# Doubled spectrum products and tap diagonals read by quadrants from PSUM in a fused S4 convolution and mixture-of-experts kernel

## The chip, the cores and the metric

One core of one Trainium2 chip. The metric is the device time of one execution in microseconds (us); "span" is the time from the first to the last instruction in the profile and is 1.8 to 2.1 us shorter in these runs. Engines: PE (TensorE matmul), PEld (its weight loads), DVE (VectorE), ACT (ScalarE), POOL, SP. The record calls a run slow when it is over 1.5% above the fastest of its kernel; all figures below are medians or means of the fast runs.

## The reference, cut to what matters

```python
g = sigmoid((x * gate_w).sum(-1, keepdims=True))      # x: 2048 tokens, 512 channels
a = ssm(x)                                            # S4: long convolution, one kernel per channel
b = moe(x)                                            # top-2 tokens go through one gated MLP
return g * a + (1 - g) * b

def ssm(u):                                           # D = 512 channels, N = 128 states
    logdA = exp(log_dt)[:, None] * (A_re + 1j * A_im)
    K  = einsum("dn,dnl,dn->dl", C, exp(logdA[:, :, None] * arange(2048)), dt * B).real
    Yf = rfft(pad(u)) * rfft(pad(K))                  # length 4096
    return irfft(Yf)[:2048] + u * Dskip
```

The kernel works on the channels in two halves of HC = 256, and each half in NG = 64 groups of four channels. A half passes through these stages:

- **Tables** of powers of the discretised A are made on DVE and ACT.
- **Taps**: for each group two matmuls (real and imaginary table) give a 128 x 84 tile. Its rows are 32 values of s for each of 4 channels, its columns 21 slots for each of 4 channels. Only the *diagonal* is wanted, where row and column belong to the same channel (the index c4).
- **Spectrum of K** ("Kh") by matmul from the diagonal rows, then eviction from PSUM.
- **Products** of the spectra of K and of u (X) on DVE, sums, folds, and the inverse transform on PE.

## The kernel before

A view `t(BF, p0, np, col, (stride, n), ...)` is: type, first partition, number of partitions, first column, then pairs of stride and count. `g.op(name, {engine: (code, cost)}, reads, writes)` records an operation. At build time a list scheduler in the kernel turns the operations into one fixed issue order per engine, by priorities from a table (ORDER), engine choices from another (ENGINE) and the order in which tiles get their addresses (PLACE).

```python
# taps: six groups to a PSUM bank, then one wide eviction
hh.matmul(o, tT1[h](BF, 0, 128, gr * 128, (1, 128)), ..., start=True, stop=False)
r = hh.matmul(o, tTI[h](BF, 0, 128, gr * 128, (1, 128)), ..., start=False, stop=True)
# ... (cut)
g.op("ev tap ...", {ACT: ..., DVE: ...})            # 128 x 1008 from PSUM to tKA, bf16

# selection: a 0/1 matrix picks the diagonal of tKA and puts it into rows 32*qd + s
for c4 in range(4):
    for qd, s in enumerate(slots):
        r = hh.matmul(ps(F32, 32 * qd, 32, (tl - tl0) * 256 + c4, (4, NG)), tSM(BF, 0, 128, 256 + 32 * c4, (1, 32)),
                      tKA(BF, 0, 128, s * 4 + c4, (84, NG)), start=True, stop=True, tile_position=(0, 32 * qd))
# ... and two more evictions, "ev kc" and "ev kd", into tKC

# products: one operation for each pair of a K part and an X part
def prod(nm, kb, kri, b, xri):                       # kri, xri: 0 = real, 1 = imaginary
    t = T(nm, NE * 2); bt = Buf(t)
    tt(nm, lambda: f4(t), lambda: k4(kb, kri), lambda: xw(b, xri), ALU.mult,
       bKH[h][kb * 4 + kri * 2:kb * 4 + kri * 2 + 2] + bX[b][xri], [bt], cd(NE), bias)
    return t, bt
```

The list before the output buffer `[bt]` says what a product has to wait for: half of a spectrum, either the real or the imaginary part.

## Time and profile before

| | before |
|---|---|
| device time | 163.69 us (163.63 to 163.76) |
| profiled execution | span 163.2 us, device time 164.97 us |
| DVE busy | 149.9 us, 228 instructions |
| PE busy | 146.2 us, 1574 matmuls |
| ACT busy | 123.8 us, 242 instructions |

"Busy" is the time in which at least one instruction of the engine runs. The profiled execution was 1.3 us slower than the timed ones. The lines of this profile stand in the prediction. One line of its DVE timeline (start, length, engine, line, operation, count) is added: the last stretch of products and folds, 73 of them.

```profile
107.29 48.95 DVE L664 TENSOR_TENSOR RB<-RB 128x2048 bf16<-128x2048 bf16 x73
```

### The profile page before, as it was taken

The numbers are of one execution on the slowest core, as the hardware profiler recorded it, in microseconds if no ns is written. First come the engines' busy times: TensorE is split into PE (matmuls) and PEld (weight loads), VectorE is DVE, ScalarE is ACT, GpSimd is POOL, SyncE is SP. The second block draws the span as 40 slices with busy tenths as digits, with TensorE's granted clock in tenths as the row PEclk, the third lists the DMA queues.
The fourth block names the chain that finished last, engine by engine and source line by source line (L and its number), as shares of the span: only waits on it lengthen the run. The fifth ranks groups of instructions, "written<-read, shape, count | busy, mean of one in ns | idle before, by whom it ended". The sixth has DMA issues, their size and how long they took to land.

```text
span 163.2 us, 3756 instructions
## 1 busy us (share of the span) xinstructions
PE 146.2 (90%) x1574; PEld 102.4 (63%) x1574; DVE 149.9 (92%) x228; ACT 123.8 (76%) x242; POOL 4.2 (3%) x12
## 2 busy tenths in 40 slices
PE   0588899999799999849999999999999999999991
PEld 0443545464334457748555679998588888888880
DVE  0499999999999999999998999999999999999933
ACT  3698999999998998999998989974751602562352
POOL 5000000000000000000100000000000000000000
PEclk9999999999999999858999999999999999999999
DMA  4899600000000996596152504858000000044044
GB/s 148 257 378 416 209 7 0 4 4 0 0 0 3 324 352 227 187 349 242 39 222 38 221 4 159 359 181 335 2 0 6 0 0 4 0 129 133 0 129 129
DMA packets 13300, 21.19 MB, mean 130 GB/s; under 512 B 2018, under 2 KB 10980, under 8 KB 12516
## 3 DMA queue, kind: packets, MB, share of 16 engines
q1 hardware_dynamic: 12996, 20.93, 37.2%
q8 instruction: 12, 0.20, 0.5%
q10 hardware_dynamic: 288, 0.03, 0.1%
q14 instruction: 4, 0.03, 0.1%
HBM read 18.86 MB, written 2.10 MB: 128 GB/s over the span
## 4 chain that ended last, share of the span: by engine, by line
PE 57%; ACT 20%; DVE 16%; DMA 3%; SPq 1%; issue 1%; DVEq 0%
PE RP L1253 17%; PE RP L958 14%; DVE RB L664 10%; PE RP L788 6%; ACT RB L851 6%; ACT RB L768 5%; ACT RB L689 5%; PE RP L844 4%; PE RP L925 4%; DMA RB<-in_A_B_re_dram 3%; PE RP L1250 2%; ACT RB L990 2%; PE RP L1227 2%; PE RP L1147 2%; DVE RB L686 2%; PE RP L898 1%
## 5 line engine op out<-in xcount | busy, mean ns | idle before, releaser
L664 DVE TENSOR_TENSOR RB<-RB 128x2048 bf16<-128x2048 bf16 (+4 forms) x103 | 83.0, 870 | 1.3 <-ACT RB L792 0.8
L844 PE MATMUL RP<-RB 128*128 128x512 bf16 x128 | 31.3, 380 | 2.8 <-ACT RB L851 1.4
L1253 PE MATMUL RP<-RB 128*128 128x256 bf16 x256 | 32.0, 273 | 0.0
L1253 PEld LDWEIGHTS RP<-RB 128*128 128x128 bf16 x256 | 25.0, 98 | 3.0 <-issue 0.2
L958 PE MATMUL RP<-RB 128*128 128x256 bf16 x208 | 25.0, 273 | 0.0
L963 ACT ACTIVATE RB<-RP 128x1024 bf16<-128x1024 f32 x14 | 14.2, 1042 | 13.7 <-PE RP L958 13.7
L708 DVE TENSOR_TENSOR RB<-RB 128x2048 bf16<-128x2048 bf16 x20 | 23.8, 1218 | 0.1
L958 PEld LDWEIGHTS RP<-RB 128*128 128x128 bf16 x208 | 20.1, 98 | 4.5 <-issue 0.2
L844 PEld LDWEIGHTS RP<-RB 128*128 128x128 bf16 x128 | 11.7, 97 | 17.6 <-ACT RB L851 3.3
L1266 ACT ACTIVATE RB<-RP,RB 128x256 bf16<-128x256 f32 x28 | 10.8, 487 | 12.0 <-DVE RB L664 5.5
L792 ACT ACTIVATE RB<-RP 128x512 bf16<-128x512 int16 x32 | 18.4, 610 | 1.5 <-PE RP L788 1.3
L768 ACT ACTIVATE RB<-RP 128x256 bf16<-128x256 f32 x62 | 18.9, 507 | 0.0
L851 ACT ACTIVATE RB<-RP 128x1024 bf16<-128x1024 f32 x15 | 15.4, 1079 | 0.4 <-PE RP L847 0.3
L788 PE MATMUL RP<-RB 128*128 128x512 bf16 x56 | 15.5, 380 | 0.0
L898 PE MATMUL RP<-RB 128*128 128x84 bf16 x128 | 11.8, 213 | 3.5 <-DVE RB L664 3.1
L898 PEld LDWEIGHTS RP<-RB 128*128 128x128 bf16 x128 | 11.2, 105 | 4.0 <-DVE RB L664 3.2
L710 DVE TENSOR_TENSOR RB<-RB 128x1024 bf16<-128x1024 bf16 x20 | 13.4, 683 | 0.0
L899 PE MATMUL RP<-RB 128*128 128x84 bf16 x128 | 11.8, 212 | 0.0
L899 PEld LDWEIGHTS RP<-RB 128*128 128x128 bf16 x128 | 11.3, 105 | 0.0
L689 ACT ACTIVATE RB<-RB 128x512 bf16<-128x512 int16 x16 | 9.1, 626 | 0.5 <-DVE RB L686 0.5
L913 ACT ACTIVATE RB<-RP 128x1008 bf16<-128x1008 f32 x9 | 9.0, 1046 | 0.0
L1250 PE MATMUL RP<-RB 128*128 128x256 bf16 x32 | 8.8, 274 | 0.0
(106 smaller groups left out, 161.1 us busy)
## 6 DMA issues: line engine op xcount, KB each, us to landing
RB<-in_A_u_dram SPq DMA_DIRECT2D x4, 1024.0 KB, 6.0
RB<-c_kspec SPq DMA_DIRECT2D x6, 512.0 KB, 4.6
RB<-c_fwd SPq DMA_DIRECT2D x4, 512.0 KB, 9.1
RB<-c_inv SPq DMA_DIRECT2D x2, 1024.0 KB, 6.6
RB<-in_B_w_up_dram SPq DMA_DIRECT2D x2, 896.0 KB, 6.9
RB<-in_B_w_gate_dram SPq DMA_DIRECT2D x2, 896.0 KB, 6.0
RB<-in_B_w_down_dram SPq DMA_DIRECT2D x2, 896.0 KB, 6.1
out_dram<-RB SPq DMA_DIRECT2D x6, 256.0 KB, 2.4
```

The source lines that it names most:

```text
L664: return g.op(name, {DVE: (lambda h: h.tensor_tensor(out=o(), in0=a(), in1=b(), op=op), cost)}, rd, wr, bias=bias, **kw)
L689: s1.append(g.op("sin z%d.%d" % (t, hh_), {ACT: (lambda h, ta=ta, i=i, hh_=hh_: h.activation(out=tZ[hh_](BF, 0, 128, i * 512, (256, 2), (1 ...
L708: g.op("%s.m%d" % (name, i), {DVE: (lambda h, i=i: h.tensor_tensor(out=ts[i](BF, 0, 128, 0, (n, 2), *like), in0=a_(), in1=b_(i), op=ALU.mu ...
L768: e2.append(g.op("exp t1_%d %d" % (h, m), {ACT: (lambda hh, m=m, s=s, h=h: hh.activation(out=tT1[h](BF, 0, 128, s * 4, (128, NG), (1, 4)), ...
L788: r = hh.matmul(ps(F32, 0, 128, 0, (1, 512)), tAM(BF, 0, 128, 1 * 128, (1, 128)), tU8(BF, 0, 128, (x * 2 + h) * HC, (0, 2), (1, HC)), star ...
L792: sins.append(g.op("sin%d %d.%d" % (h, q, cs), {ACT: (lambda hh, ps=ps, cs=cs, tt_=tt_, q=q: hh.activation(out=tt_(BF, 0, 128, 8 * q, (4, ...
L844: r = h.matmul(o, tF(BF, 0, 128, (((eo * 2 + ri) * 4 + j // 2) * 4 + ft) * 128, (1, 128)), tU(BF, 0, 128, (b * 8 + j) * D, (1, D)), start= ...
L851: g.op("ev X%d.%d.%d" % (b, ri, pr), {ACT: (lambda h, ps=ps, b=b, pr=pr, ri=ri: h.activation(out=eov(b, ri, 2 * pr, (1, 1024)), in_=ps(F32 ...
L898: hh.matmul(o, tT1[h](BF, 0, 128, gr * 128, (1, 128)), t2v(h, 0, 0, (HC, NSL), (1, 4)) if gr == 0 else tT2[h](BF, 0, 128, 4 * gr, (HC, NSL ...
L899: r = hh.matmul(o, tTI[h](BF, 0, 128, gr * 128, (1, 128)), tT2[h](BF, 0, 128, NSL * HC + 4 * gr, (HC, NSL), (1, 4)), start=False, stop=True)
L958: r = hh.matmul(o, tKM[m](BF, 0, 128, c, (1, 128)), tKC[h](BF, 0, 128, u * 256, (1, 256)), start=(n == 0), stop=(n == len(steps) - 1))
L1253: r = hh.matmul(o, tG(BF, 0, 128, ((j * 2 + ri) * 4 + ft) * 128, (1, 128)), SD(hb, ri, ft), start=False, stop=(fin and k == 1 and ft == r0 ...
```

## The change

Its intent is to shorten both full engines: fewer and larger DVE products, no selection on PE. The parts are: (1) a product takes the real and the imaginary part of K at once (and, with them, both parts of X); (2) the weights of the taps are read at stride 4, so that the rows of a tap tile are ordered by channel first, and each diagonal is then one quadrant (32 partitions) of PSUM that ACT or DVE copies straight into its rows; (3) the selection and its evictions go; (4) each of four table products (the D products) is split in two; (5) loads at the start are reordered; (6) a new ORDER, ENGINE and PLACE. Cut to its core:

```diff
-        g.dma("ld id", ..., eng=ACT, first=0)
-        g.dma("ld ldt", ..., eng=ACT, first=1)
+        g.dma("ld id", ..., eng=ACT, first=1)
+        g.dma("ld ldt", ..., eng=ACT, first=0)
...                                                  # B_re: SP queue -> ACT queue
-                            hh.matmul(o, tT1[h](BF, 0, 128, gr * 128, (1, 128)), ...)
+                            hh.matmul(o, tT1[h](BF, 0, 128, gr // 4 * 512 + gr % 4, (4, 128)), ...)
...                                                  # PSUM: 3 chunks of 24, 20 and 20 groups, 4 banks each
-                    g.op("sel %d.%d" % (h, tl), {PE: ...})       # 176 matmuls; ka table, kc and kd evictions
+                for c4 in range(4):
+                    src = lambda qd, ...: ps(F32, 32 * c4, 32, qd * 4 + c4, (16, 5 + (qd == 0)), (512, 4), (84, n))
+                    dst = lambda qd, ...: tKC[h](BF, 32 * qd, 32, c4 * NG + g0, (256, 5 + (qd == 0)), (n, 4), (1, n))
+                    def exa(hh, src=src, dst=dst):
+                        for qd in range(4):
+                            r = hh.activation(out=dst(qd), in_=src(qd), func=ACTF.Copy)
+                        return r
...                                                  # exv: the same with tensor_copy on DVE
-                        ab.append((prod(nm + "a", 0, 0, blk, xs_[0]), prod(nm + "b", 0, 1, blk, xs_[1])))
+                            tt(nm + ("ab", "cp")[kb], ...(NE, 2), (NE // 2, 2), (1, NE // 2)),
+                               ... ALU.mult,
+                               bKH[h][kb * 4:kb * 4 + 4] + bX[b][0] + bX[b][1], [bq[kb]], cd(2 * NE), bias)
```

## The prediction

> **What bounds the kernel now.** I read the page's busy shares first, then the table of engines by stretch (its columns: stretch, length, then busy us and instruction count of PE, PEld, DVE, ACT, POOL, then clock, DMA share, GB/s), then the waits of each engine, the groups by form, and the chain.
>
> ```profile
> PE 146.2 (90%) x1574; PEld 102.4 (63%) x1574; DVE 149.9 (92%) x228; ACT 123.8 (76%) x242; POOL 4.2 (3%) x12
> 0.00:7.74 7.74, 1.68 (x15) 1.42 (x16) 1.39 (x3) 3.60 (x7) 2.32 (x6) 1.00 0.68 193
> 7.74:48.00 40.26, 36.67 (x273) 18.53 (x271) 40.26 (x65) 39.33 (x77) 0.31 (x1) 1.00 0.29 107
> 48.00:79.20 31.20, 27.41 (x399) 18.73 (x399) 30.70 (x58) 29.69 (x69) 0.73 (x3) 0.89 0.64 220
> 79.20:107.29 28.09, 28.07 (x354) 20.26 (x355) 26.86 (x29) 26.99 (x51) 0.83 (x3) 1.00 0.42 151
> 107.29:156.24 48.95, 48.95 (x506) 41.02 (x504) 48.91 (x74) 22.20 (x39) 0.00 (x0) 1.00 0.19 66
> 156.24:163.20 6.96, 3.39 (x36) 2.44 (x33) 1.75 (x5) 1.94 (x5) 0.00 (x0) 1.00 0.53 151
> ```
>
> The reader is to see two full engines. From 7.74 to 156.24 us the vector engine (DVE) idles 148.50 - (40.26 + 30.70 + 26.86 + 48.91) = 1.77 us. ACT is nearly as full until 107 and more than half idle after. PE is full from 79 on. What DVE waits for is all at the two ends:
>
> ```profile
> DVE RB L607 <- ACT RB L605: 4.2, 1, 4.2
> DVE RB L1271 <- PE RP L1253: 2.6, 1, 2.6
> DVE RB L644 <- PE RP L621: 1.1, 1, 1.1
> DVE RB L659 <- PE RP L621: 1.0, 1, 1.0
> DVE RB L664 <- ACT RB L792: 0.8, 2, 0.6
> ```
>
> So the time is: 6.36 us of start-up idle (4.23 + 1.13 + 1.00), about 147 us of DVE work nearly without a gap, and 6.96 us from the last DVE fold (156.24) to the end. PE is a second bound of the same height over the last half; the chain follows PE alone from 79.2 to 158.8 because PE was never idle there. Both must get shorter for the time to fall much.
>
> The costs come from the groups by form:
>
> ```profile
> L664 DVE TENSOR_TENSOR RB<-RB 128x2048 bf16<-128x2048 bf16 x49 | 58.0, 1218 | 1.1 <-ACT RB L792 0.6 <-ACT RB L963 0.3
> L664 DVE TENSOR_TENSOR RB<-RB 128x512 bf16<-128x512 bf16 x32 | 12.0, 416 | 0.0
> L664 DVE TENSOR_TENSOR RB<-RB 128x1024 bf16<-128x1024 bf16 x16 | 10.4, 682 | 0.0
> L768 ACT ACTIVATE RB<-RP 128x256 bf16<-128x256 f32 x62 | 18.9, 507 | 0.0
> L925 PE MATMUL RP<-RB 128*32 128x64 bf16 x176 | 6.8, 300 | 0.0
> ...
> L914 DVE CAST RB<-RP 128x336 bf16<-128x336 f32 x2 | 1.0, 503 | 0.0
> ```
>
> Means are durations; consecutive instructions overlap. In the timeline two 2048-element products take 2.35-2.36 us, so a second one adds 1.135; two of 1024 take 1.28 (0.60 added); six of 512 in another line take 2.09 (0.335 added). This is a straight line: **0.068 us fixed plus 0.521 ns an element**. It also fits with dependences: 25 x 1.135 + 16 x 0.60 + 32 x 0.335 = 48.7 us against the 48.95 us measured for the 73 operations that close the kernel. From PSUM in f32 a DVE copy takes 1.04 ns an element (1008 elements: 1201 ns; 336: 503). For ACT, eighteen L768 instructions in a row take 5.08 us: about 0.278 us for 256 elements, 0.065 fixed plus 0.833 ns an element, although they read PSUM with a stride of 128 words. So strided reading costs ACT no rate here.
>
> **What the Trainium skill says.** "VectorE: DVE Perf Modes", section "The TRN2 errata — SBUF-src ops pay a fixed extra latency per instruction", says that a large tile pays the fixed cost once and many small ones pay it each time. The trace agrees in kind; the exposed share here is 0.068 us, less than the roughly 150 cycles of the page's single-operation figure, because operations overlap. The same page, "Side-by-side: where the cycles go for N=2048 bf16", puts a two-input product at about 1224 ns in the 2x mode; the trace has 1218, so merging products can't raise the rate. "SBUF — State Buffer", "Door 1: The DMA port swizzle" (its note on cachelines), lets an engine stride up to 8 bf16 elements at full rate; the new table's weights have stride 4. "TensorE: Matmul & The Clock Gate", "Weight-path perf modes", says that fast weight load reads its chunks "packed or strided". The trace of before has only packed weights for this stage (105 ns a load, hidden: pairs of taps start 38 ns apart at full clock), so whether stride 4 is free is not yet seen.
>
> **The change, part by part.**
>
> 1. *Doubled products.* Per half and block, pairs of products with the same X become one instruction over a joined K pair, and where block 1 has two terms the two combinations become one. Instructions: block 0 of each half 6 to 4, saved 2 x 2 = 4; half 0 block 1 8 + 3 to 4 + 2, saved 5; half 1 block 1, three parts, each 8 + 6 to 4 + 4, saved 18. That is 27 x 0.068 = **-1.84 us of DVE**; the elements are the same. All of it lies in DVE's full stretch.
> 2. *D products split in two* (their inputs are no longer one even stride): 4 more instructions, **+0.27 us of DVE**.
> 3. *No selection.* 176 matmuls go, with their bf16 table and the two evictions behind them. In the chain the first half's selection takes 1.58 + 3 x 0.59 = 3.35 us and the second's 3.06: **-6.4 us of PE**, all in its full stretch, and one PSUM-to-SBUF-to-PSUM trip less before each half's spectrum.
> 4. *Tap diagonals read by quadrant.* Per half, 12 groups of 4 instructions of 100 to 144 elements. On ACT: 4 x 0.065 + 504 x 0.00083 = 0.68 us for a group of the first chunk, 4 x 0.065 + 420 x 0.00083 = 0.61 for the others; 7.6 us a half were all on ACT, against 5.3 x 0.9 + 1.5 = 6.3 before. On DVE: 4 x 0.068 + 504 x 0.00104 = 0.80, and 0.71. The engine table puts at least seven groups on DVE (5 in the first half): 3 x 0.80 + 4 x 0.71 = 5.2 us, and I allow one more (0.7) where the order chooses. Before, DVE did 1.12 + 2 x 0.42 = 1.95 us of tap evictions. **About +4.0 us of DVE.** This is the new cost, and it eats the doubled products.
> 5. *Other moves between DVE and ACT*, from the engine table: two spectrum evictions of 1.135 us no longer fixed to DVE (I take -1.7), three X transposes of 0.60 become one or two (-0.9), copy of B to ACT (-0.6), 8u scaling to DVE (+0.34), two MoE rows to DVE (+0.8), Dskip copies (+0.5), small ones (+0.1): **-1.5 us of DVE**.
> 6. *Start-up.* log_dt is loaded first (the issue before it takes 0.4 us) and B_re comes on the second queue; today the chain's start is four issues and then 4.45 us of B_re, and DVE's third instruction, the copy of B, waits 1.00 us while ready work stands behind it. With the copy on ACT I take the first wait 0.35 us shorter and the third gone: **-1.35 us**.
> 7. *Permuted columns* in the spectrum and X evictions: the same elements; strided PSUM reads cost nothing above. **0**.
>
> Sum for DVE's work: -1.84 + 0.27 + 4.0 - 1.5 = +0.9 us. Start-up -1.35. *The tail:* after the last fold PE still had 2.5 us, held up by backlog (16 inverse matmuls at 0.109 would need 1.75, half of them ready one fold earlier). With 6.4 us less PE work there is no backlog: **-1.0 us**. *Inner idle:* of 1.77 us, 0.5 may go with the shorter chain from taps to spectra. Together 163.2 + 0.9 - 1.35 - 1.0 - 0.5 = 161.25 us of span. The runs are 0.5 above the span (163.69 against 163.2), so 161.75. The retuned order can also hide what I count in full, mainly quadrant copies put into DVE's gaps (1.1 us of idle between 85 and 99); I take 0.75 off: **161.0 us**, ratio 0.984.
>
> **The rivals.**
>
> *A. The PE bound was the real one.* For it: the chain is PE for 57% and PE never idles after 79. Then most of the 6.4 us arrives and start-up adds 1.35: 156 to 158 us. Against: in the same stretch DVE idles 0.04 us of 48.95, and its instruction stream predicts its length without any wait. PE can only shorten until DVE holds it.
>
> *B. The quadrant copies become the bound.* They are 96 small instructions, and each chunk takes half of PSUM, so the third chunk waits for the first to be emptied. ACT is at 27.0 of 28.1 us between 79 and 107. If the first half's 12 groups lie on the path, they need about 8 us on one engine or 4.5 on two, against 3.35 of selection and 6.3 of evictions before. Then DVE waits for its first spectrum and the time is 163 to 165. Against: DVE has had fill-in work there (second half's tables).
>
> *C. Strided weights load slower.* 256 loads; at some 30 ns each unhidden that is +7.7 us of PE, which takes back the selection's gain, and the result is near 162-163. For it: taps leave only 38 ns between matmuls. Against: the skill's two places above.
>
> **Range and chances.** My sum has two wide terms: DVE's share of the quadrant copies (+-1.5 us, since the order decides it) and how far idle and tail shrink (+-1). With the rivals on both sides, 158.2 to 163.8. Faster by over 2% means below 160.4: 0.38, for rival A in part or a better order than I can read off. Within 2%: 0.57. Slower by over 2% (above 167): 0.05, which would need B and C together.
>
> **What would show it.** Right: no 128x64 matmuls; DVE products of 4096 elements near 2.29 us each (0.15 + 4096 x 0.000521); a DVE instruction count up slightly, since 28 or more copies replace 27; DVE busy still about 150 us and no idle over 1 us between its first spectrum product and last fold; DVE continuous from about 6.4 us; PE with visible idle after 80. Wrong: DVE idle of several us at the first spectrum product (B), weight loads above 105 ns or taps more than 38 ns apart at full clock (C), DVE busy below 147 with the time below 159 (the retuning moved more work to ACT than I read), or PE still without idle and the time reduced by its 6 us (A).

## The result, and the profile after

**174.56 us** (173.94 and 175.18), 6.7% slower: ratio 1.0671 (95% interval 1.0602 to 1.074). A ratio compares the fast runs of two kernels from the same rounds by their means, so it is not quite the ratio of the medians.

The page's busy line, and three rows of the table by stretch, with the same columns as in the prediction:

```profile
PE 140.6 (82%) x1391; PEld 98.0 (57%) x1398; DVE 154.3 (90%) x233; ACT 130.8 (76%) x294; POOL 4.2 (2%) x12
72.00:80.00 8.00, 3.87 (x49) 3.65 (x51) 7.88 (x15) 6.23 (x19) 0.56 (x2) 0.50 0.96 347
80.00:88.00 8.00, 6.45 (x76) 3.93 (x75) 5.76 (x19) 5.69 (x19) 0.31 (x1) 0.94 0.47 160
88.00:96.00 8.00, 5.61 (x57) 3.62 (x55) 5.78 (x11) 6.93 (x19) 0.00 (x0) 1.00 0.74 277
```

PE is busy 5.6 us less, as intended. But from 80 to 96 us no engine is full: DVE is busy 11.5 of 16 us, PE 12.1, ACT 12.6. They wait for each other. The five longest items of what DVE waits for (total, times, longest):

```profile
DVE RB L602 <- DMA RB<-c_small: 3.9, 1, 3.9
DVE RB L918 <- PE RP L900: 2.4, 2, 1.9
DVE RB L659 <- ACT RB L945: 1.9, 1, 1.9
DVE RB L659 <- ACT RB L794: 1.4, 2, 1.0
DVE RB L639 <- PE RP L616: 1.1, 1, 1.1
```

L918 is DVE's quadrant copies waiting for taps, L659 the products waiting for evictions by ACT (L945 evicts the spectrum of K, L794 that of u). Last the groups by form: the doubled product, and the copies on ACT (L913) and DVE (L918), with their mean durations in ns after the busy time.

```profile
L659 DVE TENSOR_TENSOR RB<-RB 128x4096 bf16<-128x4096 bf16 x9 | 20.3, 2286 | 0.6 <-PE RP L900 0.6
L913 ACT ACTIVATE RB<-RP 32x100 bf16<-32x100 f32 x36 | 8.8, 245 | 0.4
L913 ACT ACTIVATE RB<-RP 32x120 bf16<-32x120 f32 x27 | 7.1, 261 | 1.2 <-PE RP L900 0.8
L918 DVE CAST RB<-RP 32x120 bf16<-32x120 f32 x13 | 3.6, 278 | 2.6 <-PE RP L900 2.4
```

Here busy time is count times duration: 36 x 245 ns = 8.8 us. So the copies never overlap. For the evictions from which the prediction took its ACT cost, it was otherwise: 62 of 507 ns each were busy for 18.9 us together, 0.30 each.

**Where the 8.6 us of span went**, by the prediction's own account of DVE (start, work, idle inside, tail; work is the page's busy time less the 1.75 us of outputs after the last fold):

| | before | after | difference | predicted |
|---|---|---|---|---|
| waits at the start | 6.36 | 5.0 | -1.4 | -1.35 |
| DVE work up to the last fold | 148.15 | 152.55 | +4.4 | +0.9 |
| idle between | 1.7 | 9.0 | +7.3 | -0.5 |
| from the last fold to the end | 6.96 | 5.2 | -1.7 | -1.0 |

The last fold ends at 159.19 + 7.38 = 166.57 us after (the timeline's last stretch of DVE) and at 156.24 before; idle is what is left of that.

### The profile page after: what moved, and what is told of

Read it like the earlier page. It is cut to its first block, busy times and chain, and to the rows that moved or that the text cites. A ratio compares the mean times of both kernels' runs of the same rounds, so it can differ in the third digit from the quotient of the medians.

```text
span 171.8 us, 3457 instructions
## 1 busy us (share of the span) xinstructions
PE 140.6 (82%) x1391; PEld 98.0 (57%) x1398; DVE 154.3 (90%) x233; ACT 130.8 (76%) x294; POOL 4.2 (2%) x12
## 4 chain that ended last, share of the span: by engine, by line
PE 42%; ACT 37%; DVE 15%; issue 2%; DMA 2%; ACTq 0%; DVEq 0%
PE RP L1218 13%; PE RP L940 11%; ACT RB L913 9%; DVE RB L659 5%; ACT RB L770 5%; ACT RB L684 5%; PE RP L790 5%; ACT RB L853 4%; PE RP L846 4%; ACT RB L972 3%; ACT RB L1017 3%; DVE RB L710 3%; DVE RB L712 2%; ACT RB L676 2%; PE RP L1129 2%
## 5 line engine op out<-in xcount | busy, mean ns | idle before, releaser
L659 DVE TENSOR_TENSOR RB<-RB 128x2048 bf16<-128x2048 bf16 (+5 forms) x76 | 81.6, 1128 | 4.6 <-ACT RB L945 1.9
L846 PE MATMUL RP<-RB 128*128 128x512 bf16 x124 | 31.1, 379 | 3.0 <-ACT RB L853 1.7
L1218 PE MATMUL RP<-RB 128*128 128x256 bf16 x256 | 31.8, 273 | 0.3 <-DVE RB L659 0.3
L940 PE MATMUL RP<-RB 128*128 128x256 bf16 x208 | 24.2, 273 | 2.9 <-ACT RB L913 2.9
L899 PE MATMUL RP<-RB 128*128 128x84 bf16 x128 | 12.3, 215 | 9.7 <-ACT RB L770 5.3
L913 ACT ACTIVATE RB<-RP 32x120 bf16<-32x120 f32 (+2 forms) x68 | 17.3, 254 | 3.5 <-PE RP L900 2.5
L710 DVE TENSOR_TENSOR RB<-RB 128x2048 bf16<-128x2048 bf16 x16 | 19.1, 1216 | 0.0
L770 ACT ACTIVATE RB<-RP 128x256 bf16<-128x256 f32 x62 | 18.9, 512 | 0.0
L945 ACT ACTIVATE RB<-RP 128x1024 bf16<-128x1024 f32 x15 | 15.1, 1026 | 4.7 <-PE RP L940 4.7
L794 ACT ACTIVATE RB<-RP 128x512 bf16<-128x512 int16 x32 | 17.7, 598 | 0.5 <-PE RP L790 0.4
L853 ACT ACTIVATE RB<-RP 128x1024 bf16<-128x1024 f32 x15 | 15.8, 1067 | 0.4 <-PE RP L849 0.4
L790 PE MATMUL RP<-RB 128*128 128x512 bf16 x56 | 14.9, 380 | 0.9 <-ACT RB L794 0.9
L900 PE MATMUL RP<-RB 128*128 128x84 bf16 x128 | 12.3, 215 | 0.0
L918 DVE CAST RB<-RP 32x120 bf16<-32x120 f32 (+2 forms) x28 | 7.6, 272 | 2.9 <-PE RP L900 2.4
```

Of the source, the lines that this page charges most:

```text
L659: return g.op(name, {DVE: (lambda h: h.tensor_tensor(out=o(), in0=a(), in1=b(), op=op), cost)}, rd, wr, bias=bias, **kw)
L710: g.op("%s.m%d" % (name, i), {DVE: (lambda h, i=i: h.tensor_tensor(out=ts[i](BF, 0, 128, 0, (n, 2), *like), in0=a_(), in1=b_(i), op=ALU.mu ...
L770: e2.append(g.op("exp t1_%d %d" % (h, m), {ACT: (lambda hh, m=m, s=s, h=h: hh.activation(out=tT1[h](BF, 0, 128, s * 4, (512, 16), (128, 4) ...
L790: r = hh.matmul(ps(F32, 0, 128, 0, (1, 512)), tAM(BF, 0, 128, 1 * 128, (1, 128)), tU8(BF, 0, 128, (x * 2 + h) * HC, (0, 2), (1, HC)), star ...
L794: sins.append(g.op("sin%d %d.%d" % (h, q, cs), {ACT: (lambda hh, ps=ps, cs=cs, tt_=tt_, q=q: hh.activation(out=tt_(BF, 0, 128, 8 * q, (4, ...
L846: r = h.matmul(o, tF(BF, 0, 128, (((eo * 2 + ri) * 4 + j // 2) * 4 + ft) * 128, (1, 128)), tU(BF, 0, 128, (b * 8 + j) * D, (1, D)), start= ...
```

## The experiments

Eleven kernels ran; all passed the comparison with the reference. My theory H after the result was: the copies are *held*. The Trainium skill, "VectorE: DVE Perf Modes", section "Two Vector instructions with no wait between them", gives a model in which a Vector instruction whose output starts in another quadrant than the last output (or whose input starts in another one than the last input) starts only when every earlier one has finished. I had read other sections of that page before predicting and missed this one. The rivals: the form of the copies is slow in itself (F), the tuned order of the change is bad for the costs that copies really have (O), the doubled products wait for more than before (W), and the first taps wait for a PSUM bank (B).

### Copies that stay in one quadrant

The change as it is, in its own order, but each copy writes into the quadrant that it reads. The rows are wrong on purpose (the comparison didn't notice, so it says nothing about these rows).

```diff
-  src = ... (16, 5 + (qd == 0)) ...
-  dst = ... tKC[h](BF, 32 * qd, 32, c4 * NG + g0, (256, 5 + (qd == 0)), (n, 4), (1, n))
+  src = ... (16, 5 + (qd == 0 and c4 != 2)) ...
+  dst = ... tKC[h](BF, 32 * c4, 32, (c4 + qd) % 4 * NG + g0, (256, 5 + (qd == 0 and c4 != 2)), (n, 4), (1, n))
```

> The changed kernel with its own order; each of the four tap copies of a group now writes the quadrant that it reads (in other columns), so no copy of a group moves to another quadrant; same counts, same access patterns, a wrong result on purpose. Theory H (a copy that writes another 32-partition quadrant than the one before it is held until that one has finished): copies of a group start about 0.165 us apart on ACT instead of 0.26-0.28, and about 0.20 on DVE instead of 0.27-0.30; their durations stay 0.25-0.30; the time falls by 4 to 7 us, to 167-170. Rival F (the cost lies in the form, 32 partitions and a four-level pattern): spacing stays 0.26-0.30 and the time stays 173.5-175. Rival O (the order, not the copies, makes the loss): spacing may fall, but the time falls by less than 2 us.

Measured: 168.18 us (167.43 to 168.41), ratio 1.0253 (1.021 to 1.0295). That is 6.4 us less than the change. Timeline of the change, then of this kernel: eight copies on ACT, eight on DVE, and the second half's forty on ACT.

```profile
79.50 2.23 ACT L913 ACTIVATE RB<-RP 32x144 bf16<-32x144 f32 x8 [1.73 <-PE RP L900]
80.37 2.40 DVE L918 CAST RB<-RP 32x144 bf16<-32x144 f32 x8
111.51 10.74 ACT L913 ACTIVATE RB<-RP 32x144 bf16<-32x144 f32 x40
```

```profile
79.32 1.50 ACT L913 ACTIVATE RB<-RP 32x144 bf16<-32x144 f32 x8 [1.73 <-PE RP L900]
80.19 1.82 DVE L918 CAST RB<-RP 32x144 bf16<-32x144 f32 x8
109.51 7.18 ACT L913 ACTIVATE RB<-RP 32x144 bf16<-32x144 f32 x40
113.69 47.32 DVE L659 TENSOR_TENSOR RB<-RB 128x4096 bf16<-128x4096 bf16 x48
```

The elements are the same but for one column block in one copy of sixteen, and the duration of one copy is nearly so (32x100 on ACT: 233 ns against 245). What changed is the pitch, from start to start: 0.268 us to 0.18 on ACT, 0.30 to 0.23 on DVE, with every fourth copy still changing quadrant. H is shown, for ACT as well as for DVE, and F is refuted.

The edit did a second thing: each copy now reads and writes the same quadrant, which three of four in the change do not. The single records of the two traces decide between the two. In this run a copy starts, within a group of four, 90 to 99 ns before the end of the one in front of it on ACT, and 70 to 76 on DVE. The first copy of a group, which also reads and writes one quadrant, but another one than the copy in front of it, starts 23 to 31 ns after that one's end. In the change every copy in a row starts 11 to 32 ns after it, also the one of four that reads and writes the same quadrant. So it is the change of quadrant from copy to copy that holds, not a shift within a copy.

The last line answers to the 48.95 us x73 of before: 48 operations in 47.32 us. Both move 83,968 elements a partition. Twenty-five fewer took 1.63 us less, 0.065 each, where the prediction had 0.068.

### The change in another order

All operations of the change, with the measured costs of the copies, and ORDER, ENGINE and PLACE from a new search (a random search over priorities with a cost estimate fitted to the profile).

```diff
-ORDER, ENGINE, PLACE of the change
+ORDER, ENGINE, PLACE found with copies at 0.245 to 0.30 us each
```

> The changed kernel, every operation kept, with another issue order, engine choice and SBUF placement, searched for with copy durations as the trace of the changed kernel shows them. Theory O (the order that came with the change is a poor one once the copies cost what they do): 163-166 us, 8 to 11 us below the changed kernel, and DVE idle inside the kernel falls from over 5 us to under 3. Theory H alone (the copies cost what they cost in any order): at most 4 us below, 170 or more.

Measured: fast runs of 165.33 to 165.8 us (a slow one of 168.6 left out), ratio 1.0108 (1.0073 to 1.0144). So 9.0 us of the loss go with the order, the engine choices and the placement alone, although every copy is still held. O is shown. How the order does it is shown in part only. It is not the row of held copies before the second half's spectrum: this kernel has 36 of them in a row too (9.59 us), and so has the fast run of the quadrants alone below (9.67 us). What went away are DVE's waits: the last 48 products and folds run 47.25 us without a gap, where the change waits 0.55, 1.87 and 0.56 us within them, and from 80 to 96 us DVE is busy 14.9 us instead of 11.5. The profile fell into the slow execution, so these figures say which waits are gone, not how long anything takes.

### Both: new order and copies in one quadrant

The last order with the first experiment's edit; the rows are wrong again.

> The reordered kernel of e2 with the edit of e1 (each group of four copies stays in the quadrant that it reads; the tap rows are wrong on purpose). If the hold and the order are separate losses that add: 3 to 6 us below e2, 160 to 163 us. If the reordering has already put the held copies where they cost nothing: within 1.5 us of e2, 164 to 166.

Measured: 162.9 us (162.66 to 163.5; a slow run of 165.87 left out), ratio 0.9948 (0.988 to 1.0015). Here is the whole list of what DVE waits for down to 0.4 us, and its last stretch:

```profile
DVE RB L601 <- ACT RB L599: 3.7, 1, 3.7
DVE RB L653 <- PE RP L615: 1.6, 1, 1.6
DVE RB L1235 <- PE RP L1217: 0.8, 1, 0.8
DVE RB L658 <- PE RP L848: 0.4, 1, 0.4
```

```profile
108.32 47.20 DVE L658 TENSOR_TENSOR RB<-RB 128x4096 bf16<-128x4096 bf16 x48
```

Between its first two waits and its last fold (108.32 + 47.20 = 155.52 us) DVE idles about 1.0 us in all, 0.4 of it in one wait. PE is busy 141.2 us, 5 us less than before, and it buys nothing. DVE binds, as the prediction said; but even with cheap copies DVE is busy 151.0 us against 149.9. What the merged products save is less than what the copies and other moves add. So the change, in the best order tried and with copies that are not held but go to wrong rows, only reaches the time of the kernel before.

### Only the doubling, and only the quadrants, each in a searched order

```diff
 e3: kernel before + doubled products and the layout of X by halves;   new ORDER, ENGINE, PLACE
 e4: kernel before + stride-4 weights, quadrant copies, no selection;  new ORDER, ENGINE, PLACE
```

> The kernel before with only the spectra by halves and the doubled products (selection and start-up as before), order searched for anew. If the prediction's term holds (27 instructions x 0.068 us): 161 to 162.5 us, and DVE products of 4096 elements with 2.29 us each, 2.20 apart. If the merged products bring nothing: 163.5 or more.

> The kernel before with only the first table in fours, the quadrant reads and no selection (products undoubled, start-up as before), order searched for anew with measured copy durations. Theory H: the quadrant copies add about 10 us of ACT and DVE work and save 6.4 us of PE that DVE can't use: 164.5 to 167.5, slower than before. Rival (PE was the bound, so the selection's 6.4 us arrive): 158 to 162.

Measured: the doubling alone 165.58 us, ratio 1.01 (1.0041 to 1.0159), a miss against my expectation; the quadrants alone 167.71 us (166.87 to 169.29), ratio 1.0251 (1.0188 to 1.0314: slower, though whether by over 2% is unclear). The busy line of the second:

```profile
PE 140.5 (85%) x1390; PEld 97.7 (59%) x1398; DVE 154.5 (94%) x251; ACT 128.4 (78%) x301; POOL 4.2 (3%) x12
```

PE's saving of 5.7 us is all there (140.5 against 146.2), and DVE went up 4.6 us to 154.5. In this order the quadrant part is a net loss by itself. A searched order is a second change, though, so I ran the search's control:

```diff
 e11: kernel before, no edit;  new ORDER, ENGINE, PLACE from the same search
```

> Control for the kernels that were run in a newly searched order (the reordered change, the doubling alone, the quadrants alone): the kernel before, no edit at all, in an order from the same search with the same costs. The search's own estimate falls from 161.7 to 159.3 us of span for it. If the estimate can be trusted at that grain, the time is 161 to 161.5 us. Rival: for the doubling alone the estimate was 160.6 and the span measured was 162.4 to 163.7, so the search finds what the estimate leaves out, and the time is 163 to 166; then a searched order costs 2 us by itself, and the two single parts can't be judged to within that.

Measured: 163.65 us (163.0 to 164.87; a slow run of 166.71 left out), ratio 1.0006 (0.9898 to 1.0115), though the search had estimated 2.4 us less. A searched order is about as good as the kernel's own, within 1.2%, and its estimate is 2 us or more too low. The interval of the quadrants' loss (from 1.0188) lies above that of this control (to 1.0115); the doubling's 1% does not, and that needed a test in a fixed order.

### The doubling in the order of the kernel before

Every engine keeps the sequence of the kernel before; a doubled product stands where the later of its two parts stood.

```diff
-  Y..a = K.re * X.re ;  Y..b = K.im * X.im          # each at its own place
+  Y..ab = (K.re, K.im) * (X.re, X.im)               # at the place of the later one
```

> The kernel before with its own issue order kept instruction by instruction; only the spectra by halves and the doubled products are put in, each doubled product at the place of the later of the two that it replaces. Theory W (a doubled product needs the real and the imaginary part of a spectrum at once, so DVE must wait for the second part where a single product could begin on the first): new DVE waits for the spectrum evictions on ACT, about 3 us before the first half's products and 3 to 4 us before the second half's, and 167 to 170 us in spite of 27 fewer DVE instructions. Rival (the fixed cost saved is all there is to it): 161 to 162.5 us and no new wait over 0.5 us.

Measured: 168.54 us (168.43 to 168.61), ratio 1.0285 (1.0219 to 1.0351), 5 us slower with 27 fewer DVE instructions (201 against 228) and DVE busy 148.6 us. Its DVE timeline has two waits where the kernel before had none:

```profile
108.09 21.62 DVE L696 TENSOR_TENSOR RB<-RB 128x4096 bf16<-128x4096 bf16 x13 [2.36 <-ACT RB L996]
132.02 28.41 DVE L696 TENSOR_TENSOR RB<-RB 128x1024 bf16<-128x1024 bf16 x36 [2.31 <-ACT RB L996]
```

L996 evicts the spectrum of K. Both waits stand at the start of a half's products. In the kernel before, the products of the part of K that is out already stand there. W is shown for this order: the doubling saves 1.3 us of busy time on DVE (149.9 to 148.6) and opens 4.7 us of waits.

### Doubling only where both parts are there

In the same order again, only the six late pairs (c and d) of the last block are doubled and its twelve first sums become six; a and b stay apart. A second kernel has only the start-up loads of the change, a third has both.

```diff
 e9:   Y1.1p*.c and Y1.1p*.d -> one doubled product; Y1.1p* and Y1.1p*cd -> one sum (12 instructions fewer)
 e8:   log_dt first on the ACT queue, then the identity, then B_re (was on the SP queue)
 e10:  e8 and e9 together
```

> The kernel before in its own order, doubling only where both halves of the spectrum have been there for long: in the second half's block 1 the six pairs of products with the second block of the spectrum (c and d) become six doubled ones, and the twelve first combinations become six. That is 12 of the change's 27 saved instructions, 0.8 us of vector work. The products a and b stay apart, because before uses b early, while the real part of the spectrum is still on its way. Theory W (doubling costs where it has to wait for the second part): here no new wait over 0.6 us, and the time is 163 to 164 instead of the 168.5 of the full doubling. Rival (doubled products are slow in themselves, or the layout by halves of X is what cost the 5 us): 166 or more. I do not expect the 0.8 us to show in full, because TensorE has no idle after 79 us and the last fold only comes earlier if its transforms do.

> The kernel before in its own order, with one thing of the change: log_dt is loaded first on the second queue, ahead of the identity, and B_re follows there instead of coming fifth on the first queue. (The copies of B stay where they were.) The prediction's step 6: the vector engine's third wait (1.00 us) goes and the first is 0.35 shorter, and everything behind starts that much earlier: 162.2 to 162.6 us. Rival: the later bound (TensorE's stretch from 79 us on) is set by something that doesn't start earlier, such as a load, and the time stays at 163.5. In the trace: vector engine waits at the start of about 3.9 and 1.1 us and no third one.

> The two edits of the kernels run beside it together (start-up loads, and doubling only where both parts are ready), still in the order of the kernel before. If the start-up is the only thing that moves the time: 162.2 to 162.6, like the start-up alone; if the saved 0.8 us of vector work counts too: 161.5 to 162.

Measured, with 163.59 us for the kernel before in these rounds: e9 163.42 us (ratio 0.9965, 0.9923 to 1.0006), e8 163.33 (0.9959, 0.9922 to 0.9997), e10 163.43 (0.9961, 0.9924 to 0.9999). The two long spectrum waits of the full doubling are gone in e9. Of the 1.1 us left, 0.33 is a wait that the kernel before has too, and 0.72 is new, a little over the 0.6 expected. So neither the doubled product nor the layout by halves was slow in itself. But the 0.8 us less of DVE work (148.9 busy against 149.7 in e8) hardly show. The last stretch of e9:

```profile
105.91 29.41 DVE L697 TENSOR_TENSOR RB<-RB 128x2048 bf16<-128x2048 bf16 x31
136.04 18.92 DVE L697 TENSOR_TENSOR RB<-RB 128x2048 bf16<-128x2048 bf16 x30 [0.72 <-ACT RB L997]
```

From 105.91 to the last fold these 61 operations take 49.05 us, as long as the 73 of e8, which have no gap (49.05). DVE comes earlier to a part of the spectrum that ACT has not evicted yet, and this one wait takes back what the merging saved. What DVE waits for in e9:

```profile
DVE RB L640 <- ACT RB L638: 4.2, 1, 4.2
DVE RB L1345 <- PE RP L1327: 2.5, 1, 2.5
DVE RB L677 <- PE RP L654: 1.1, 1, 1.1
DVE RB L697 <- ACT RB L997: 1.1, 2, 0.7
```

This list has a second message (its 2.5 us at the end are nothing new: 2.6 before). The start of e9 is that of the kernel before, unedited, and there is no third wait of 1.00 us. DVE's first instructions in e9:

```profile
4.19 0.69 DVE L640 TENSOR_TENSOR RB<-RB 128x512 bf16<-128x512 bf16 x1 [4.19 <-ACT RB L638]
6.01 0.69 DVE L677 TENSOR_SCALAR RB<-RP 128x512 f32<-128x512 f32 x1 [1.13 <-PE RP L654]
6.62 0.68 DVE L692 COPY RB<-RP 128x512 f32<-128x512 f32 x1
```

The copy of B (L692) starts at 6.62; in the profile of before it starts at 7.74 and waits 1.00. So that wait belonged to the one profiled execution, whose B_re came late (PE waits 1.1 us for that load in it) and which took 164.97 us instead of 163.7. The doubling in the kernel's own order, with the same start, has no such wait either. The start-up edit alone gives 0.26 us by the medians and not 1.35. (Its ratio says 0.4%, because three of the eleven runs of the kernel before in these rounds came out 1 us or more above the others.) So e8 is the fastest version with right rows, by very little, and e9 and e10 add nothing to it.

### The first taps without the PSUM bank

In the change, the first taps need four banks, and one of them is read by ACT (L770, exponentials) to the last moment. Here those exponentials read a copy in SBUF; the order is that of the change.

```diff
+  cp A: tAS <- A_ps[0]      # 128 x 512, ACT
-  exp t1 ...: in_=A_ps[0](F32, 0, 128, h * NG, (4, 16), (128, 4), (1, 4))
+  exp t1 ...: in_=tAS(F32, 0, 128, h * NG, (4, 16), (128, 4), (1, 4))
```

> The changed kernel in its own order with one ACT copy more (0.6 us near 10 us), so that the second half's exponentials read A from SBUF and no longer hold one of the four PSUM banks that the first tap chunk needs. Theory B (the four-bank chunks make the first taps wait for a bank): the first taps start 1.5 to 2 us earlier, right after the first half's table is done, and their wait for the exponentials (5.3 us of PE idle) becomes 3.5 us for DVE. If that wait is on the path: 172 to 173.5 us. If the three chunks that follow in the same four banks set the pace or DVE has other work: unchanged, 174 to 175.5.

Measured: 175.62 us (174.76 to 177.31), ratio 1.0729 (1.0638 to 1.082): nothing gained. The first tap in the change, and here:

```profile
75.91 0.26 PE L899 MATMUL RP<-RB 128*128 128x84 bf16 x1 [5.30 <-ACT RB L770]
```

```profile
75.90 0.26 PE L933 MATMUL RP<-RB 128*128 128x84 bf16 x1 [3.30 <-DVE RB L691]
```

The tap starts at the same time and now names a product of the table on DVE as what it waited for. The wait for the bank had stood in front of a wait for data of the same end. B is refuted. (Here PE did other matmuls just before, hence 3.30 and not 5.30. This profile is of a run 1.5% above the fastest.)

## Why the prediction was wrong

**The failed step is part 4**, "Tap diagonals read by quadrant": "4 x 0.065 + 504 x 0.00083 = 0.68 us for a group" on ACT and 0.80 on DVE. Both take the pitch of copies that overlap. The 96 copies are held at each change of quadrant and cost their whole duration: 0.268 us on ACT instead of 0.165, and 0.30 on DVE for one of the first chunk instead of 0.20. On DVE the 28 copies took 2.40 + 2.21 + 1.08 + 1.18 + 1.09 = 7.96 us of the timeline, where the prediction had 5.2 for these seven groups, and 5.9 with an eighth that did not come; on ACT the second half's forty took 10.74 us, where 6.1 to 6.8 for ten groups would have been expected. Undoing the hold gives back 6.4 us in the change's order and 2.5 in the better one. (The reading of the ACT line was also a little off: eighteen evictions in 5.08 us, the last with its whole 0.507, give a pitch of (5.08 - 0.507) / 17 = 0.269 us and not 0.278.)

**The step after it failed with it**: "0.5 may go" of inner idle. Idle grew by 7.3 us. The prediction took the new order as tuned for the real costs. It wasn't: the same operations run 9.0 us faster in another order.

**Part 1 counted only what it saves.** The 27 instructions and 0.068 us each were right (DVE's last stretch: 1.63 us less for 25; a doubled product 2286 ns against 2.29 predicted). That a product then waits for both parts was not looked at, though the list of what it reads is in the diff. In the order of before it costs more than it saves.

**Part 3 was right in size and worth nothing.** PE's busy time fell by 5.6 us against 6.4 predicted. The argument against rival A, that PE can only shorten until DVE holds it, is what the reordered kernel with cheap copies shows.

**Part 6 rested on one execution.** Its -1.35 us even agrees with the difference of the two profiles, but that is luck: 1.00 of it is a late load in one run. The 0.35 at the first wait came (4.2 us before, 3.82 in e8); alone the edit gave 0.26. For the same reason "The runs are 0.5 above the span" was wrong: 163.69 and 163.2 belong to different executions, and the offset within that execution is 1.8 us (164.97 to 163.2). The two errors cancel in the sum (163.2 + 0.5 is the median), so this cost the prediction nothing; the 1.00 us did.

**The tail** shrank as predicted: 5.2 us after the last fold, 1.7 less than before, against 1.0. (A DVE that waits also gives PE time to catch up, but in the reordered kernel with cheap copies, where DVE hardly waits, the tail is 5.2 us too: 160.7 - 155.52.)

**The rivals.** B ("The quadrant copies become the bound") had the right mechanism and was given 163 to 165, because it used the same cost of a copy and left the second half out. Its "DVE idle of several us at the first spectrum product" came: 1.87 us before the second half's products, and 2.4 us at the first half's taps. C's sign came, but not its cost: a weight load of stride 4 takes 119 to 120 ns against 105, but in the second half, at full clock, taps start 39 ns apart against 38 before (medians), so nearly all of the 15 ns is hidden.

**What stays open.** I can't split the 9.0 us of the order between its waits; no run moved one of them alone. Part 5, the moves between the engines, was not tested by a run: DVE's work grew by 4.4 us where 0.9 was predicted, and the copies explain 2.1 of the difference. The groups by form of the two profiles place 1.1 of the remaining 1.4: only one spectrum eviction left DVE (1.1 us, not 1.7), and three small operations of 256 columns, whose access pattern the change permutes, take longer (two subtractions 610 ns against 417, a copy 378 against 282): 0.5 us that the prediction left out. A copy whose *read* quadrant changes while the written one stays was not tried.

## What to carry to other kernels

Before many small copies are priced from a pitch in the trace, ask whether they would overlap as those did: take the duration as the cost where start quadrants change. Ordering the copies so that they change seldom is the obvious next try; no run here did it with right rows. Merging two operations into one also merges what they wait for, so count for each merged instruction which input comes last and what filled the time until then. A merging that saves work can also just turn it into a wait, as in e9. And before a wait is booked as a gain, look for it in a second execution.

## What the Trainium skill lacked or had wrong

- ScalarE copies are held like VectorE's when the quadrant written changes: forty copies of 100 to 144 elements took 10.74 us with a change at every copy and 7.18 with one at every fourth, at nearly the same duration of one. A held copy costs about 0.12 us more (of 120 elements: pitch 0.273 against 0.152). "ScalarE: Activation LUTs" doesn't mention it; the model of "VectorE: DVE Perf Modes" is for Vector instructions.
- "VectorE: DVE Perf Modes", section "Two Vector instructions with no wait between them", agrees with these runs: eight copies from PSUM took 2.40 us with the change of quadrant and 1.82 with most of it removed. The page gives the rule but no cost; here a held copy costs about 0.10 us more (of 120 elements: pitch 0.298 against 0.203).
- "SBUF — State Buffer", section "Door 1: The DMA port swizzle", and "TensorE: Matmul & The Clock Gate", section "Weight-path perf modes", led me to expect strided weights to be free. A load of stride 4 took 119 to 120 ns against 105 packed, and nearly all of it was hidden: matmuls of 84 columns started 39 ns apart against 38. No page gives the longer load.
